# One order table for another: resequencing a fused attention and snake-MLP kernel

## The chip, the cores and the metric

The kernel runs on one core of one Trainium2 chip. The metric is device time in microseconds (us) of one execution; the number given for a kernel is the median over runs. TensorE, VectorE, ScalarE, GpSimd and SyncE appear as PE, DVE, ACT, POOL and SP; each works through its own instructions in order.

## The reference

Block-decayed linear attention (4 batches, 8 heads, 768 tokens, head size 64), whose output becomes the 3072 x 512 input of an MLP with a "snake" activation:

```
out_block   = (q k^T * Dmask) v + (q * lam_pow) @ kv_state     # per batch, head, block of tokens
kv_state    = lam_block * kv_state + (k * rev_pow)^T v
x           = out, heads side by side                          # 3072 x 512
h = x @ w_in                                                   # 512 -> 2048
s = sin(alpha * h)
g = h + s * s / (alpha + 1e-09)
return g @ w_out                                               # 2048 -> 512
```

All inputs and the result are float32; the kernel computes in bf16 with float32 accumulation.

## The kernel before, in words

Tokens are worked in six groups t = 0..5 of 128 tokens for all four batches, so a group is a 512-wide column block for the MLP. What a group needs is cut into small steps, and the whole body after a fixed preamble is a hand-held list of such steps, the string `ORDER` (line 14 on). A loop at line 491 reads the string word by word and records each step; nothing reorders them afterwards. A word is a letter, the indices (group first), and after a colon the PSUM banks that the step takes. Each engine's instruction stream is therefore the words in the string's order, filtered by the engine.

The letters, with the line of each function and its engine:

- `I1`..`I3` load a quarter of w_in (two DMAs each, L141) and `W0`..`W3` a quarter of w_out (one DMA each, L145). All are issued by POOL. The first quarter of w_in is loaded in the preamble (L187, four DMAs).
- `r` and `R` load raw k and raw q of a group (four DMAs each, L124), `n` and `v` load k and v in their natural layout (two DMAs each, L131), all issued by POOL. `d` decays k (L260) and `z` scales raw q (L264): POOL arithmetic. `C` casts the first state (L287, POOL).
- `k` and `j` turn raw k and raw q (L240, DVE). `F` computes scores into four banks (L249, PE), `m` masks one of them (L255, DVE). `K` computes state updates (L274, PE), `S` folds them in (ACT for group 0, L281; DVE otherwise, L283), `B` casts the state (L287, ACT). `O` computes attention outputs in four banks (L295, L304, PE), `x` copies one bank out as the MLP's input (L314, ACT).
- `h g.f:bank` is one of 16 "hidden" steps of a group: four 128x512 matmuls (L325). `s` takes the sine (L330, ACT). The square is `q` on ACT (L336), `Q` on DVE as a product (L338), or `P` on DVE as a fused form (L340). `t` finishes with a multiply-add into `gall` on DVE (L345), which also frees the bank.
- `u g.m.part:bank` is a quarter of an output projection: four matmuls (L352), of which part 0..3 uses the quarter 0..3 of w_out. `o` copies the finished bank out (ACT, L358) and stores it (SP, L360).

After the loop, line 494 calls `project_halves(5, 3)` (L362), which does the last projection in two halves of 256 columns, so that the first half is copied and stored while the second is computed.

Two things set what waits for what. PSUM has eight banks, and a step that names a bank waits for the reader of the bank's last content. And POOL's DMAs are recorded on eight semaphores in turn: a DMA issue carries a wait for the landing of the eighth DMA before it, and an issue that waits holds up whatever stands behind it on POOL. `raw_k` and `raw_q` have one buffer each, the natural k and v two each, the sine and the square four each, the output staging tile three.

Of the kernel before, what the change touches and what calls it, by code (L numbers as in the profile page):

```python
# [21 lines left out]
m1.0.1 u0.0.2 m1.0.2 u0.1.2 m1.0.3 r2 F1.1:2736 u0.3.1 m1.1.0 m1.1.1 u0.2.2 m1.1.2 u0.3.2 m1.1.3 O1:2736 v2  # L22
u0.0.3 x1.0 x1.1 u0.1.3 x1.2 x1.3 u0.2.3 z2.0 o0.0 o0.1 h1.0:2 o0.2 h1.1:7 s1.0 z2.1 j2.0 h1.2:3 q1.0 k2.0 s1.1
h1.3:6 s1.2 n1 t1.0 h1.4:4 q1.1 k2.1 q1.2 u0.3.3 s1.3 t1.1 s1.4 h1.5:5 n2 t1.2 o0.3 h1.6:0 q1.4 P1.3 s1.5 t1.4
F2.0:2713 s1.6 t1.3 r3 h1.7:4 q1.5 m2.0.0 q1.6 h1.8:6 m2.0.1 s1.7 m2.0.2 u1.0.0:2 q1.7 m2.0.3 s1.8 d1.0 u1.1.0:7
t1.5 q1.8 h1.9:1 t1.6 t1.7 d1.1 h1.10:3 s1.9 t1.8 h1.11:5 q1.9 j2.1 s1.10 h1.12:0 d2.0 s1.11 t1.9 q1.10 K1:46
s1.12 t1.10 h1.13:1 d2.1 q1.12 S1.0 h1.14:3 s1.13 S1.1 B1.0 u1.0.1 t1.12 B1.1 R3 q1.13 Q1.11 K2:46 t1.11 s1.14
h1.15:0 t1.13 q1.14 u1.1.1 S2.0 s1.15 v3 u1.0.2 t1.14 q1.15 B2.0 S2.1 F2.1:5143 t1.15 B2.1 u1.1.2 m2.1.0 n3
u1.0.3 m2.1.1 m2.1.2 z3.0 u1.1.3 o1.0 m2.1.3 u1.2.0:6 o1.1 k3.0 O2:0514 z3.1 j3.0 k3.1 u1.3.0:2 x2.0 x2.1 j3.1
u1.2.1 x2.2 x2.3 F3.0:3705 h2.0:1 m3.0.0 m3.0.1 h2.1:4 s2.0 m3.0.2 h2.2:3 q2.0 m3.0.3 s2.1 t2.0 h2.3:7 s2.2 d3.0  # L30
u1.3.1 q2.1 q2.2 t2.1 h2.4:0 s2.3 t2.2 d3.1 h2.5:5 q2.3 s2.4 t2.3 h2.6:1 s2.5 r4 q2.4 K3:43 q2.5 t2.4 h2.7:7
s2.6 t2.5 h2.8:0 q2.6 S3.0 R4 s2.7 h2.9:5 t2.6 B3.0 s2.8 h2.10:4 Q2.7 t2.7 s2.9 h2.11:1 S3.1 q2.8 v4 q2.9 u1.2.2
t2.8 B3.1 t2.9 h2.12:7 s2.10 k4.0 s2.11 u1.3.2 n4 q2.10 k4.1 u1.2.3 q2.11 s2.12 u1.3.3 t2.10 o1.2 t2.11 q2.12
z4.0 F3.1:3054 o1.3 t2.12 u2.0.0:6 m3.1.0 h2.13:1 m3.1.1 z4.1 u2.0.1 m3.1.2 s2.13 m3.1.3 h2.14:2 j4.0 O3:7305
s2.14 Q2.13 q2.14 t2.13 t2.14 u2.0.2 x3.0 d4.0 j4.1 x3.1 h2.15:4 x3.2 x3.3 F4.0:1273 s2.15 d4.1 h3.0:0 m4.0.0
q2.15 m4.0.1 h3.1:5 s3.0 t2.15 h3.2:1 q3.0 m4.0.2 s3.1 t3.0 K4:24 s3.2 m4.0.3 u2.0.3 q3.1 S4.0 q3.2 h3.3:7 t3.1
# [21 lines left out]
def kernel(  # L58
# [273 lines left out]
    def square(g, f, eng):  # L332
        s_sb = s_of.pop((g, f))
        s2_of[g, f] = mlps.tile([P, GRP], BF16, name="s2")
        if eng is A:
            A.activation(out=s2_of[g, f][:], in_=s_sb[:], func=ACTF.Square)  # L336
        elif eng is V:
            V.tensor_tensor(out=s2_of[g, f][:], in0=s_sb[:], in1=s_sb[:], op=ALU.mult)  # L338
# [9 lines left out]
    def project(g, m, part, n):  # L348
        if part == 0:
            ops[g, m] = bank("ops", n)  # L350
        for f in range(4 * part, 4 * part + 4):
            nc.tensor.matmul(out=ops[g, m][:], lhsT=gall[g][:, f, m * P:(m + 1) * P],  # L352
                             rhs=w_out_sb[part][:, f % 4, :],
                             start=(f == 0), stop=(f == NFC - 1))
# [170 lines left out]
```

## Time and profile before

| what | value |
|---|---|
| median of 3 runs | 211.4 us (210.08, 211.40, 212.85) |
| the profiled execution: its own time | 212.47 us |
| the profiled execution: span from first to last instruction | 210.8 us |
| PE busy | 197.1 us (94%) |
| ACT busy | 148.1 us (70%) |
| DVE busy | 135.7 us (64%) |
| POOL busy | 100.8 us (48%) |
| POOL's DMA queue: packets, bytes | 63184, 15.47 MB |

The profile is of one execution. Its own time is 1.7 us longer than its span (what lies around the first and the last instruction), and 1.1 us above the median of the three runs. Times in it count from the start of the span. Busy shares are averages over stages: the first 17 us are the preamble, in which PE turns and scores group 0 and waits for k, q, v and the first weights; then the MLP of group 0 runs while the weights still land; from about 53 us the steps of all later groups are mixed. For PE, 0.86 us is four 128x512 matmuls back to back at full clock, so one `h` or one `u` step. A matmul's listed duration (about 380 ns) contains the filling of the array and overlaps its neighbour's.

### The profile page before, as it was taken

What the parts mean: (1) busy time and instruction counts of PE and PEld (TensorE: products, weight loads), DVE (VectorE), ACT (ScalarE), POOL (GpSimd) and SP (SyncE); (2) the same over time, 40 slices, a digit from 0 to 9 for tenths busy, and PEclk for the clock granted to TensorE, in tenths of its full rate; (3) what the DMA queues carried; (4) which work ended last, traced back from release to release, by engine and by line L of the source; (5) the groups of instructions that cost most, each with busy time, mean ns of one, the idle gap of its engine ahead of it and who ended that gap; (6) DMA issues with size and microseconds to landing.
All of it is one profiled execution on the core that took longest, in us unless ns stands there. A gap on an engine that the chain in (4) does not pass through costs nothing.

```text
span 210.8 us, 4860 instructions
## 1 busy us (share of the span) xinstructions
PE 197.1 (94%) x1992; PEld 97.7 (46%) x2021; DVE 135.7 (64%) x201; ACT 148.1 (70%) x258; POOL 100.8 (48%) x116
## 2 busy tenths in 40 slices
...
GB/s 124 156 151 182 205 193 162 165 197 166 229 165 166 77 145 183 48 142 157 157 75 166 116 53 50 51 2 0 53 50 50 0 100 35 70 16 33 0 105 98
DMA packets 68920, 22.61 MB, mean 107 GB/s; under 512 B 50834, under 2 KB 65954, under 8 KB 68898
## 3 DMA queue, kind: packets, MB, share of 16 engines
q0 software_dynamic: 63184, 15.47, 79.6%
...
q14 instruction: 6, 0.05, 0.1%
...
## 4 chain that ended last, share of the span: by engine, by line
PE 74%; DMA 11%; DVE 5%; POOL 4%; ACT 2%; issue 2%; DVEq 0%; ACTq 0%; POOLq 0%
PE ops L352 35%; PE hps L325 29%; DMA w_in<-in_moe_w_in_dram 4%; DMA w_out<-in_moe_w_out_dram 4%; DMA nat_k<-in_k_dram 3%; PE F_ps L249 3%; PE O_ps L304 2%; DVE gall L345 2%; POOL nat_k L260 2%; DVE STm L255 2%; PE hps L367 2%; PE O_ps L295 2%; POOL w_in L141 1%; DVE S L283 1%; PE T_ps L387 1%
## 5 line engine op out<-in xcount | busy, mean ns | idle before, releaser
L345 DVE SCALAR_TENSOR_TENSOR gall<-s,r_sb,hps 128x512 bf16<-128x512 bf16 x96 | 69.3, 742 | 46.9 <-ACT s L336 36.8
L325 PE MATMUL hps<-xt,w_in 128*128 128x512 bf16 x372 | 90.9, 379 | 2.0 <-issue 0.7
L352 PE MATMUL ops<-w_out,gall 128*128 128x512 bf16 x352 | 88.1, 382 | 4.0 <-DMA w_out<-in_moe_w_out_dram 2.4
L330 ACT ACTIVATE s_sb<-hps,alpha_sb 128x512 bf16<-128x512 f32 x96 | 64.2, 692 | 27.7 <-PE hps L325 27.5
L325 PEld LDWEIGHTS <-w_in 128*128 128x128 bf16 x384 | 36.7, 98 | 46.0 <-issue 2.2
L352 PEld LDWEIGHTS <-gall 128*128 128x128 bf16 x368 | 35.1, 98 | 44.8 <-issue 3.7
L336 ACT ACTIVATE s<-s_sb 128x512 bf16<-128x512 bf16 x86 | 52.9, 638 | 1.6
L255 DVE TENSOR_TENSOR STm<-F_ps,C 128x512 bf16<-128x512 f32 x40 | 25.0, 683 | 4.2 <-PE F_ps L249 4.1
L260 POOL TENSOR_TENSOR nat_k<-nat_k,R 128x1024 bf16<-128x1024 bf16 x10 | 19.1, 1933 | 4.5 <-DMA nat_k<-in_k_dram 4.4
L264 POOL TENSOR_TENSOR raw_q<-raw_q,Rraw 128x1024 bf16<-128x1024 bf16 x10 | 18.9, 1919 | 4.0 <-DMA raw_q<-in_q_dram 4.0
L314 ACT CAST xt<-O_ps 128x512 bf16<-128x512 f32 x20 | 10.3, 600 | 14.9 <-PE O_ps L304 14.5
L358 ACT COPY o_sb<-ops 128x512 f32<-128x512 f32 x23 | 13.5, 592 | 8.0 <-PE ops L352 6.2
L240 DVE STREAM_TRANSPOSE turned_q<-raw_q 128x512 f32<-128x512 f32 x10 | 11.1, 1114 | 5.6 <-POOL raw_q L264 5.6
L131 POOL DMA_DIRECT2D nat_v<-in_v_dram x12 | 14.0, 1170 | 0.2 <-issue 0.2
L124 POOL DMA_DIRECT2D raw_k<-in_k_dram x20 | 11.7, 598 | 3.9 <-DMA w_out<-in_moe_w_out_dram 2.9
L124 POOL DMA_DIRECT2D raw_q<-in_q_dram x20 | 11.6, 588 | 4.0 <-DMA w_in<-in_moe_w_in_dram 2.6
L131 POOL DMA_DIRECT2D nat_k<-in_k_dram x10 | 11.8, 1190 | 0.8 <-POOLq L509 0.8
L240 DVE STREAM_TRANSPOSE turned_k<-raw_k 128x512 f32<-128x512 f32 x10 | 11.0, 1117 | 0.1
L338 DVE TENSOR_TENSOR s<-s_sb 128x512 bf16<-128x512 bf16 x9 | 5.9, 657 | 2.4 <-ACT s_sb L330 2.4
L249 PEld LDWEIGHTS <-turned_k 32*128 32x128 bf16 x320 | 5.0, 96 | 4.6 <-issue 3.8
L249 PE MATMUL F_ps<-turned_q,turned_k 32*128 32x128 bf16 x320 | 6.8, 224 | 0.0
L192 PE MATMUL spare<-fill 128*128 128x512 bf16 x11 | 5.0, 607 | 1.5 <-DVE one L174 1.5
...
## 6 DMA issues: line engine op xcount, KB each, us to landing
...
```

Of the source, the lines that this page charges most:

```text
L124: (eng or G).dma_start(out=dst[quad[a], bs].rearrange("t b n r d -> t (b n) (r d)"), in_=src[t, a])
L131: G.dma_start(out=nat[nm, t][:, bs].rearrange("p b h e -> p (b h) e"), in_=SRC[nm][bs, :, t * T:(t + 1) * T, :].rearrange("b h p e -> p (b ...
L240: V.transpose(out=dst.rearrange("p (x t r) -> p x r t", r=R, t=32), in_=src.rearrange("p (x r d) -> p x r d", r=R, d=32))
L249: nc.tensor.matmul(out=F[a][:, u, n, :], lhsT=KQ["k", t][quad[a], 2 * pr + u, n, :, e], rhs=KQ["q", t][quad[a], 2 * pr + u, n, :, e], star ...
L255: V.tensor_tensor(out=st[t, pr][:, a], in0=att["F", pr][a], in1=C0[:, a].unsqueeze(1).broadcast_to([P, 2, NQ, T]), op=ALU.mult)
L260: G.tensor_tensor(out=kd, in0=kd, in1=R128[:].unsqueeze(1).unsqueeze(3).broadcast_to([P, 2, H, D]), op=ALU.mult)
L264: G.tensor_tensor(out=qs, in0=qs, in1=Rraw[:].rearrange("p n r -> p (n r)").unsqueeze(1).unsqueeze(3).broadcast_to([P, 2, NQ * R, D]), op= ...
L325: nc.tensor.matmul(out=hps[g, f][:], lhsT=w_in_sb[f // 4][:, c, (f % 4) * P:(f % 4 + 1) * P], rhs=xt[g][:, c, :], start=(c == 0), stop=(c ...
L330: A.activation(out=s_of[g, f][:], in_=hps[g, f][:], func=ACTF.Sin, scale=alpha_sb[:, f:f + 1])
L336: A.activation(out=s2_of[g, f][:], in_=s_sb[:], func=ACTF.Square)
L345: V.scalar_tensor_tensor(out=gall[g][:, f, :], in0=s2_of.pop((g, f))[:], scalar=r_sb[:, f:f + 1], in1=hps.pop((g, f))[:], op0=ALU.mult, op ...
L352: nc.tensor.matmul(out=ops[g, m][:], lhsT=gall[g][:, f, m * P:(m + 1) * P], rhs=w_out_sb[part][:, f % 4, :], start=(f == 0), stop=(f == NF ...
```

## The change

`ORDER` is replaced as a whole by another list of the same steps, and the last projection becomes a step of the list (`e5.3:56`, the last word), with banks given in the word instead of 0 and 1. No instruction's shape changes. Counted over the two strings: the squares on ACT (`q`) go from 86 to 61, on DVE as a product (`Q`) from 9 to 15, on DVE in the fused form (`P`) from 1 to 20; all other letters keep their counts. The order of PE's steps and the banks differ nearly everywhere; so do POOL's steps.

POOL's steps in the order of the two strings, up to the loads of group 3:

```
before: I1 W0 d0.0 I2 d0.1 I3 r1 C0.0 C0.1 R1 W1 W2 v1 W3 z1.0 z1.1 R2 r2 v2 z2.0 z2.1 n1 n2 r3 d1.0 d1.1 d2.0 d2.1 R3
after:  d0.0 I1 I2 d0.1 r1 I3 R1 W0 W1 z1.0 W2 z1.1 v1 W3 C0.1 C0.0 r2 R2 n1 n2 z2.0 z2.1 d1.0 v2 d1.1 d2.0 R3 d2.1 r3
```

The diff, cut (the words on the left-out lines are of the same kinds):

```diff
 ORDER = """
-I1 W0 d0.0 I2 h0.0:2 d0.1 h0.1:4 s0.0 h0.2:5 s0.1 Q0.0 I3 t0.0 K0:73 s0.2 Q0.1 h0.3:6 S0.0 r1 t0.1 q0.2 C0.0
-h0.4:0 s0.3 t0.2 S0.1 h0.5:1 q0.3 h0.6:2 C0.1 s0.4 t0.3 s0.5 h0.7:7 R1 q0.4 u0.0.0:4 q0.5 t0.4 s0.6 u0.1.0:5
-t0.5 s0.7 Q0.6 h0.8:3 t0.6 h0.9:6 Q0.7 s0.8 t0.7 h0.10:0 s0.9 Q0.8 t0.8 W1 h0.11:1 s0.10 Q0.9 W2 h0.12:2 t0.9
-q0.10 s0.11 v1 t0.10 h0.13:7 s0.12 k1.0 h0.14:3 q0.11 q0.12 t0.11 h0.15:6 s0.13 W3 t0.12 s0.14 u0.2.0:0 k1.1
-q0.13 z1.0 u0.3.0:1 q0.14 t0.13 s0.15 t0.14 q0.15 z1.1 j1.0 u0.0.1 t0.15 u0.1.1 j1.1 F1.0:2736 R2 u0.2.1 m1.0.0
...
-q5.13 u5.1.0:3 t5.13 s5.14 h5.15:5 q5.14 t5.14 u5.1.1 s5.15 u5.2.0:7 q5.15 t5.15 u5.1.2 u5.0.3 u5.1.3 o5.0
-u5.2.1 o5.1 u5.2.2 u5.2.3 o5.2
+d0.0 h0.0:3 h0.1:5 h0.2:7 I1 s0.0 q0.0 s0.1 s0.2 t0.0 q0.1 I2 h0.3:6 q0.2 t0.2 h0.4:0 h0.5:1 t0.1 s0.3 s0.4 q0.3
+P0.4 d0.1 t0.4 r1 h0.6:4 h0.7:3 t0.3 s0.5 s0.6 s0.7 K0:52 S0.1 I3 P0.5 P0.6 t0.5 S0.0 R1 q0.7 t0.7 h0.8:2 s0.8
+h0.9:0 s0.9 W0 t0.6 q0.8 h0.11:6 k1.1 h0.10:7 q0.9 t0.9 s0.10 t0.8 h0.12:3 k1.0 s0.11 s0.12 q0.10 q0.11 q0.12
+h0.15:1 t0.10 t0.11 h0.13:0 s0.13 W1 h0.14:2 s0.14 t0.12 u0.1.0:7 u0.0.0:6 z1.0 j1.0 q0.13 q0.14 u0.2.0:4 t0.13
+t0.14 F1.0:2305 s0.15 q0.15 t0.15 u0.2.1 u0.1.1 W2 u0.3.0:1 u0.2.2 z1.1 j1.1 m1.0.1 m1.0.2 m1.0.3 m1.0.0
+F1.1:2530 u0.3.1 m1.1.0 v1 u0.0.1 W3 C0.1 C0.0 r2 u0.3.2 R2 m1.1.3 m1.1.2 m1.1.1 O1:2530 x1.0 x1.3 x1.1 k2.1
...
+t2.9 h2.11:1 s2.10 q2.10 t2.10 B2.1 d3.1 h2.12:4 r4 s2.11 s2.12 q2.11 u1.3.2 K3:20 k4.1 R4 m3.1.2 u1.3.3 o1.3
+h2.13:5 S3.1 O3:7360 S3.0 q2.12 t2.12 t2.11 s2.13 q2.13 u2.0.0:4 h2.14:1 z4.0 n4 j4.0 k4.0 t2.13 x3.0 x3.1 x3.2
...
+u2.1.2 k5.1 m4.1.1 s3.5 q3.5 t3.5 h3.6:4 s3.6 u2.3.1 u2.1.3 q3.6 k5.0 u2.3.2 K4:27 v5 o2.1 z5.0 O4:0136 x4.0
+t3.6 x4.3 u2.3.3 j5.1 o2.3 h3.7:0 x4.1 u2.2.0:6 S4.0 S4.1 h3.8:2 j5.0 s3.7 Q3.7 x4.2 t3.7 F5.0:1475 m5.0.0
...
+t3.11 h3.14:2 t3.12 s3.14 q3.14 B4.1 m5.1.1 t3.13 u3.0.1 u3.1.1 u3.0.2 t3.14 h3.15:0 s3.15 P3.15 u3.1.2 O5:3457
+x5.0 x5.1 x5.2 h4.3:2 x5.3 t3.15 h4.0:3 h4.5:4 s4.0 q4.0 h4.2:7 h4.1:5 s4.1 s4.2 u3.1.3 u3.0.3 o3.0 u3.3.0:0
...
+u5.0.2 s5.15 P5.15 u4.0.0:7 u5.1.1 u5.2.2 u5.1.2 t5.15 t5.14 u5.0.3 u5.2.3 o5.2 u5.1.3 o5.1 o5.0 u4.0.1 u4.0.2
+u4.0.3 o4.0 e5.3:56
 """
...
-    def project_halves(g, m):
+    def project_halves(g, m, *bks):
         for n in range(2):
             cols = slice(n * DM // 2, (n + 1) * DM // 2)
-            ps = bank("hps", n)
+            ps = bank("ops", bks[n])
...
+        "e": project_halves,
     }
     for word in ORDER.split():
         which, _, banks = word[1:].partition(":")
         STEP[word[0]](*map(int, which.split(".")), *map(int, banks))
-    project_halves(NT - 1, B - 1)
```

More of the change, by code (lines that the diff above doesn't have):

```diff
@@ L22 @@
[L22 to L36, printed above, removed]
@@ new lines @@
+t0.14 F1.0:2305 s0.15 q0.15 t0.15 u0.2.1 u0.1.1 W2 u0.3.0:1 u0.2.2 z1.1 j1.1 m1.0.1 m1.0.2 m1.0.3 m1.0.0
+F1.1:2530 u0.3.1 m1.1.0 v1 u0.0.1 W3 C0.1 C0.0 r2 u0.3.2 R2 m1.1.3 m1.1.2 m1.1.1 O1:2530 x1.0 x1.3 x1.1 k2.1
+x1.2 u0.1.2 k2.0 u0.2.3 n1 n2 u0.1.3 o0.1 o0.2 h1.0:0 s1.0 z2.0 P1.0 t1.0 h1.1:3 s1.1 z2.1 q1.1 h1.2:4 s1.2
+h1.3:2 s1.3 q1.2 t1.1 q1.3 t1.2 h1.5:7 j2.0 h1.4:5 s1.4 q1.4 t1.4 t1.3 u0.0.2 s1.5 q1.5 u0.3.3 t1.5 d1.0 u0.0.3
+j2.1 o0.3 h1.6:0 o0.0 h1.7:5 F2.0:7146 m2.0.1 m2.0.3 s1.6 h1.8:3 q1.6 s1.7 q1.7 t1.6 t1.7 h1.9:2 m2.0.0 m2.0.2
@@ new lines @@
+s1.8 s1.9 h1.15:1 q1.8 q1.9 v2 t1.8 h1.10:6 s1.10 h1.11:0 t1.9 q1.10 t1.10 h1.12:7 d1.1 K1:53 S1.0 d2.0 s1.11
+S1.1 h1.13:4 s1.12 q1.11 q1.12 u1.1.0:6 s1.13 q1.13 t1.11 R3 h1.14:5 u1.1.1 d2.1 t1.12 t1.13 s1.14 q1.14 t1.14
+F2.1:3027 m2.1.0 m2.1.1 B1.0 s1.15 m2.1.2 B1.1 q1.15 t1.15 u1.0.0:4 u1.1.2 u1.0.1 r3 K2:30 m2.1.3 u1.0.2 z3.0
+S2.1 j3.0 u1.1.3 o1.1 n3 O2:1275 x2.0 x2.2 x2.3 S2.0 x2.1 B2.0 k3.0 k3.1 u1.2.0:6 u1.0.3 u1.2.1 F3.0:2510 m3.0.0
+m3.0.3 o1.0 z3.1 v3 m3.0.2 h2.0:7 h2.1:3 s2.0 u1.2.2 m3.0.1 q2.0 t2.0 s2.1 q2.1 t2.1 h2.2:0 s2.2 j3.1 u1.2.3
@@ new lines @@
+o1.2 h2.3:5 h2.4:1 q2.2 t2.2 F3.1:2764 m3.1.0 s2.3 s2.4 h2.5:0 u1.3.0:3 h2.6:2 m3.1.3 q2.3 q2.4 t2.4 t2.3 s2.5
+m3.1.1 q2.5 t2.5 s2.6 h2.7:1 s2.7 q2.6 P2.7 t2.7 h2.8:4 s2.8 q2.8 u1.3.1 t2.6 t2.8 h2.9:7 s2.9 Q2.9 h2.10:5 d3.0
+t2.9 h2.11:1 s2.10 q2.10 t2.10 B2.1 d3.1 h2.12:4 r4 s2.11 s2.12 q2.11 u1.3.2 K3:20 k4.1 R4 m3.1.2 u1.3.3 o1.3
+h2.13:5 S3.1 O3:7360 S3.0 q2.12 t2.12 t2.11 s2.13 q2.13 u2.0.0:4 h2.14:1 z4.0 n4 j4.0 k4.0 t2.13 x3.0 x3.1 x3.2
+x3.3 u2.0.1 s2.14 F4.0:3762 m4.0.2 h2.15:0 q2.14 v4 m4.0.0 s2.15 q2.15 m4.0.1 z4.1 m4.0.3 d4.1 h3.1:5 h3.5:3
@@ new lines @@
+j4.1 h3.0:6 s3.0 s3.1 t2.15 u2.0.2 q3.0 t2.14 t3.0 h3.2:7 h3.3:2 u2.0.3 q3.1 t3.1 R5 r5 s3.2 P3.2 s3.3 q3.3
+u2.1.0:1 h3.4:6 t3.2 t3.3 B3.1 u2.1.1 o2.0 d4.0 z5.1 F4.1:4270 m4.1.3 m4.1.0 m4.1.2 s3.4 B3.0 q3.4 u2.3.0:5 t3.4
+u2.1.2 k5.1 m4.1.1 s3.5 q3.5 t3.5 h3.6:4 s3.6 u2.3.1 u2.1.3 q3.6 k5.0 u2.3.2 K4:27 v5 o2.1 z5.0 O4:0136 x4.0
+t3.6 x4.3 u2.3.3 j5.1 o2.3 h3.7:0 x4.1 u2.2.0:6 S4.0 S4.1 h3.8:2 j5.0 s3.7 Q3.7 x4.2 t3.7 F5.0:1475 m5.0.0
+m5.0.1 s3.8 Q3.8 h3.12:3 u2.2.1 t3.8 h3.9:4 s3.9 m5.0.3 u2.2.2 m5.0.2 h3.10:0 u2.2.3 B4.0 Q3.9 t3.9 s3.10 Q3.10
@@ new lines @@
+t3.10 F5.1:1524 m5.1.3 h3.13:7 o2.2 h3.11:0 s3.11 s3.12 m5.1.0 u3.1.0:6 u3.0.0:1 m5.1.2 Q3.11 Q3.12 s3.13 q3.13
+t3.11 h3.14:2 t3.12 s3.14 q3.14 B4.1 m5.1.1 t3.13 u3.0.1 u3.1.1 u3.0.2 t3.14 h3.15:0 s3.15 P3.15 u3.1.2 O5:3457
+x5.0 x5.1 x5.2 h4.3:2 x5.3 t3.15 h4.0:3 h4.5:4 s4.0 q4.0 h4.2:7 h4.1:5 s4.1 s4.2 u3.1.3 u3.0.3 o3.0 u3.3.0:0
+t4.0 q4.1 t4.1 u3.2.0:3 s4.3 P4.2 t4.2 u3.3.1 h4.6:5 h4.7:1 Q4.3 t4.3 u3.2.1 h4.4:2 s4.4 s4.5 P4.4 P4.5 t4.4
+s4.6 t4.5 s4.7 u3.3.2 u3.2.2 u3.3.3 o3.3 q4.6 t4.6 q4.7 t4.7 h4.8:7 u3.2.3 o3.2 s4.8 P4.8 h4.9:4 h4.11:2 h4.10:5
```

21 lines of the change are left out of this document (6 added, 15 removed).

## The prediction, on record before the changed kernel ran

> **What bounds the kernel now.** I read the page's chain first, then PE by stages, then the chain of the first 55 us, then POOL's timeline, last DVE's and ACT's groups.
>
> ```profile
> PE 74%; DMA 11%; DVE 5%; POOL 4%; ACT 2%; issue 2%; DVEq 0%; ACTq 0%; POOLq 0%
> ```
> ```profile
> core 0: us, PE busy (x) PEld busy (x) DVE busy (x) ACT busy (x) POOL busy (x), PEclk, DMA share, GB/s
> 16.80:52.80 36.00, 32.23 (x343) 15.28 (x350) 23.79 (x34) 19.31 (x34) 27.34 (x34) 0.95 1.43 182
> 52.80:207.50 154.70, 153.00 (x1535) 75.27 (x1555) 99.54 (x140) 118.26 (x203) 58.24 (x54) 1.00 0.69 87
> ```
> PE is the bound, and from 52.8 us on it has no slack to give: 153.0 of 154.7 us busy at full clock. What can still be won lies between 16.8, where the first hidden step starts, and 52.8. The chain there:
>
> ```profile
> 20.67 8.87 DMA w_in<-in_moe_w_in_dram
> ...
> 30.48 7.97 DMA w_out<-in_moe_w_out_dram
> 38.45 0.04 issue
> 38.49 2.37 PE ops L352 x8
> 40.85 0.97 PE F_ps L249 x27
> ```
> PE stands still for the second quarter of w_out (W1), issued at 30.5 and landed at 38.45: PE's wait is 2.39 us. The eight matmuls after it take 2.37 us and not 1.73: the clock is halved. The windows of 3.41 us around it:
>
> ```profile
> 12.45:15.87 3.42, 2.08 (x49) 1.59 (x48) 3.05 (x6) 2.49 (x5) 3.35 (x5) 1.00 1.63 155
> 36.35:39.76 3.41, 1.27 (x6) 0.58 (x6) 2.51 (x4) 0.68 (x2) 2.96 (x2) 1.00 1.29 165
> 39.76:43.17 3.41, 3.08 (x38) 1.50 (x38) 2.00 (x4) 0.00 (x0) 2.44 (x5) 0.50 2.24 168
> ```
> A stretch with PE busy for 1.27 of 3.41 us (37%) is followed by one at clock 0.50; one with 2.08 (61%) is not.
>
> ```profile
> 14.15 0.83 POOL L145 DMA_DIRECT2D w_out<-in_moe_w_out_dram  x1
> 21.27 1.76 POOL L124 DMA_DIRECT2D raw_k<-in_k_dram  x3
> 30.48 0.78 POOL L145 DMA_DIRECT2D w_out<-in_moe_w_out_dram  x1
> 31.73 0.75 POOL L145 DMA_DIRECT2D w_out<-in_moe_w_out_dram  x1 [0.47 <-issue]
> 34.74 0.78 POOL L145 DMA_DIRECT2D w_out<-in_moe_w_out_dram  x1
> 45.23 0.58 POOL L124 DMA_DIRECT2D raw_k<-in_k_dram  x1 [1.00 <-DMA nat_v<-in_v_dram]
> 47.88 0.58 POOL L124 DMA_DIRECT2D raw_k<-in_k_dram  x1 [2.08 <-DMA w_out<-in_moe_w_out_dram]
> ```
> W0 is issued at 14.2, W1 to W3 from 30.5 on. Adding each issue's start to its time to landing gives the landings: w_in quarter 1 at 21.2, W0 23.5, w_in 2 27.2, w_in 3 29.5, raw k (four) 32.2, raw q (four) 34.9, W1 38.45, W2 41.6, nat v 44.9, W3 47.6. They land in the order of issue with hardly a gap, so the queue itself is full, and the pitches are prices: w_in pair 2.3 to 3.7, four raw loads 2.7, a w_out 2.3 to 3.5, two nat_v 3.4.
>
> **PE's balance before.** By the chain's rows four 512-wide matmuls are 0.86 us. 96 hidden and 92 projection steps are 188 x 0.864 = 162.4; the halves 3.5; ten F of 0.61, five K of 0.62, five O of 1.70 give 17.7. Together 183.6. PE ends at 207.5: 207.5 - 16.8 - 183.6 = 7.1 us of loss. By the start of group 1's hidden steps (52.86) the string has 30.3 us of PE work: loss 5.8 up to there, 1.3 after. The span ends 3.3 after PE, and the execution takes 1.7 beyond its span.
>
> **The change, part by part.**
>
> *Same work on PE.* All step counts of PE are kept: 183.6 again. The preamble is untouched: start at 16.8, first w_in quarter at its old place.
>
> *POOL's issues.* W0 moves from ahead of d0.0 to behind raw q: 12 DMAs (w_in 2 and 3, eight raw loads) go past it. raw k goes ahead of w_in 3. d0.0 moves ahead of w_in 1 and delays that issue by one tensor operation, 1.9 us: 14.9 instead of 12.95, plus the shortest w_in time to landing, 5.0, is 19.9 against 19.6 for its first half, so +0.3 at most. The DMAs ahead of W2 are the same set in both strings, only shuffled: with a full queue W2 lands at 41.6 again, nat v at 44.9, W3 at 47.6. (W2 now waits on POOL behind z1.0, which waits for raw q: 32.6 + 1.9 = 34.5, and by the shortest w_out time, 8.0, that would be 42.5; range 41.6 to 42.5.) raw q's landing is the old 34.9 less W0's 2.3: 32.6. W0 follows it by 2.3 to 3.5: 34.9 to 36.1; two middle pitches of 3.1 back from W2 give 35.4, which I take, and W1 at 38.5. w_in 3 lands four raw loads before raw q's end: 29.9.
>
> *PE up to W0.* The string now puts all 16 hidden steps and K0 (14.5 us) before the first projection. The last four hidden need w_in 3: 29.9 + 3.5 = 33.4. The waits ahead of that hide under it: w_in 1 lets h0.4 start at 21.5, and four hidden, K0 (0.6), the copy S0.1 (0.6 plus handing over) that h0.8 must wait for, since it takes K0's own bank 2, and four hidden more are done at 29.8. Without w_in 3 as cover that bank's turn would cost its 0.7. PE then waits for W0 from 33.4 to 35.4: 2.0 us in place of the 2.39 for W1. ACT does not set this: 13 squares and 16 sines in pairs of about 1.16 and 1.26 us, and two copies, from 17.9 on are 18.8, done at 36.7, and the banks that u0.1.0 and u0.0.0 take are free at about 33.7.
>
> *The clock.* If that wait falls into one 3.41 us stretch, PE is busy 41% of it: nearer to the 37% that was followed by the half clock than to the 61% that was not. I take the halving; it stretches what PE does in the 3.4 us behind it by 1.7. The Trainium skill ("TensorE: Matmul & The Clock Gate", section "Why this matters for your kernels") asks only that no idle gap exceed about 3 us; by it neither 2.39 nor 2.0 should have cost clock. The trace disagrees for the 2.39.
>
> *W0 to group 1.* From 35.4 seven steps up to u0.2.2 are 5.8 us: 41.2, or 42.9 at half clock; W2 (41.6) then no longer stops PE. At u0.2.2 the string has 20.2 us of PE work: loss 42.9 - 16.8 - 20.2 = 5.9, or 4.6 unhalved (W2's 41.6). F1.1 to O1 has four masks (0.62 apart) inside three projections (2.6), as before. So 5.9 against 5.8 before.
>
> *POOL for group 2.* n1, n2 go ahead of z2, and v2, r3 behind d1. The last raw q issue of group 2 waits for the eighth DMA before it, W3 (47.6, as the 2.08 row shows), and lands about 5.1 later, 53; then z2 (3.8), d1.0, v2 (2.3), d1.1 end at 62.9. K1 is needed at 16.8 + 5.9 + 43.9 = 66.6: covered by 3.7 us. F2.0 (60.8) has its z2.0 at 54.9, K2 (73.9) its d2.1 at 69.0. No cost; if the cover went, POOL's lateness would come out on PE one for one. SP's stores keep count and order of copies.
>
> *Squares.* ACT loses 25 of 0.630: -15.8 us. DVE gains 19 fused of 0.684 and 6 products of 0.418, and no longer meets POOL's arithmetic with products (two of nine took 1.16 and 1.82): about +13.
>
> ```profile
> L338 DVE TENSOR_TENSOR s<-s_sb x9: 418/419/1824, 18.6 to 103.1; 128x512 bf16<-128x512 bf16 x9
> L345 DVE SCALAR_TENSOR_TENSOR gall<-s,r_sb,hps x96: 677/747/749, 20.4 to 198.5; 128x512 bf16<-128x512 bf16 x96
> ```
> ACT goes to 132, DVE to 149, both under PE's 190 us: nothing. The multiply-adds lie between 677 and 749 ns all 96 times, while POOL runs 1.9 us tensor operations at 20 places: the distance kept from those has nothing to win.
>
> *Bank turns later.* Counted over the strings in PE work between a bank's last write and its next use, the shortest before is 1.46 us (u1.2.3 to u2.0.0). After, three are 0.86: u1.3.3 to O3, O4 to h3.7, O5 to h4.0. The copies that free them take 0.585, and O writes its first bank 0.8 us before its end, so the lower end is 0; the upper, 1.1 each, is under the rivals. I take 0.5 together.
>
> *Tail.* The halves get banks 5 and 6, free long before; 3.3 us as before.
>
> **Sum.** Loss 5.9 + 1.3 + 0.5 = 7.7 against 7.1: +0.6 on the profiled 212.47, so 213.1. That execution stands 1.1 above its median of 211.4; put on the median, 212.0 us.
>
> **Rivals.**
>
> *No halved clock* (the wait is split over two stretches, or W0 lands at 34.9, leaving PE busy 56%): loss 4.6 + 1.8 = 6.4, 1.3 less: 210.7. That is also where the skill's 3 us rule leads. Chance 0.25.
>
> *Weights early:* W0 34.9, W2 39.6 (34.5 plus the 5.1 of the fastest raw load): loss 3.6 and 1.3, 2.2 under before: 209.2. Against it: the full queue. Chance 0.05; a gain over 2% needs 4.2 of the 7.1 and is 0.02 of it.
>
> *W0 lands where W1 did* (38.5, if raw loads are served ahead of it more slowly, POOL being late with each): 38.5 - 16.8 - 14.5 = 7.2, halving 1.7, later 1.8: 10.7, +3.6: 215.0. It decides from a landing of about 36.5. Chance 0.12, half of it over 2%.
>
> *Bank turns (the slower side).* At O3, O4 and O5 one ACT instruction stands ahead of the freeing copy. The only row of this kind before is PE's 0.4 us wait for an o_sb copy, at distances of 1.46 to 1.73; at 0.86 it would be 0.4 + 0.7 = 1.1 each, 3.3 in all; and if two such waits leave PE under some 45% of a stretch, 1.7 more: 212.0 - 0.5 + 5.0 = 216.5. The Trainium skill (same page, section "A second HAM failure mode: psum-queue depth-cycling") describes such a loss of clock through bank turns; before, from 43.2 on, the clock is 1.00 throughout. Chance 0.16, 0.10 of it over 2%.
>
> *It does not do what its name says:* W0 is issued later, not first, and the distances from POOL act on DVE, off the chain. That is inside the forecast.
>
> **How the numbers follow.** Forecast 212.0 with chance 0.42, its own range 211 to 213.5. The range 209.0 to 216.4 takes in early weights, late W0 and most of the bank turns. What a measurement here can tell is about 2%, so 207.2 to 215.6 is no change: faster 0.02, slower 0.06 + 0.10 = 0.16, same 0.82.
>
> **What would show it.** W0 landing near 35.4 and PE waiting about 2 us for w_out, now for W0; one stretch at clock 0.50 behind it; group 1's first hidden step within 1 us of 51.3 (28.6 of work, 16.8, 5.9); PE over 98% busy from there on; ACT near 132 and DVE near 149. Wrong if PE shows waits for ACT's L314 or L358 after 90 us, a second stretch at half clock, or w_out landings in another order than issued.

## The result and the profile after

| what | before | after |
|---|---|---|
| median of 22 runs each, on the same chip | 210.92 us (209.68 to 213.14) | 213.18 us (212.07 to 214.74) |
| ratio | | 1.011, 95% interval 1.0088 to 1.0131 |
| the profiled execution: its own time, its span | 212.47 us, 210.8 us | 212.93 us, 211.1 us |
| PE busy | 197.1 us | 196.5 us |
| ACT busy, DVE busy | 148.1 us, 135.7 us | 134.0 us, 148.5 us |

The changed kernel is slower by 1.1%, some 2.3 us. The forecast was 212.0 us and no change: the time lies inside the range, but it is a small loss that the runs do separate from no change. Ratios and their intervals leave out executions over 1.5% longer than the fastest of the same kernel, so a ratio need not be the quotient of the medians beside it.

The profile after is read in the order of the prediction. First the page's chain by engine, and PE by stages, cut where group 1's hidden steps are under way (the columns of a stage are given in its first line):

```profile
PE 63%; DMA 14%; POOL 12%; DVE 6%; issue 3%; ACT 1%; POOLq 0%; DVEq 0%; ACTq 0%
```
```profile
core 0: us, PE busy (x) PEld busy (x) DVE busy (x) ACT busy (x) POOL busy (x), PEclk, DMA share, GB/s
16.80:51.30 34.50, 31.71 (x341) 15.07 (x347) 21.93 (x32) 20.87 (x38) 25.31 (x32) 0.95 1.33 178
51.30:207.50 156.20, 153.56 (x1538) 75.81 (x1558) 114.18 (x168) 102.57 (x175) 60.51 (x55) 1.00 0.71 89
```

From 51.3 us on PE is busy for 153.56 of 156.20 us (98.3%). POOL now holds 12% of the chain that ended last, against 4% before. Where it stands in that chain is seen in the chain of the first 60 us (start, duration, what):

```profile
25.78 7.22 DMA raw_q<-in_q_dram
...
33.16 1.90 POOL raw_q L264
35.06 0.77 POOL w_out L145
...
35.84 1.92 POOL raw_q L264
37.76 2.28 POOL nat_v L131 x2
40.04 8.32 DMA w_out<-in_moe_w_out_dram
48.36 0.04 issue
48.41 1.89 PE ops L352 x8
50.29 5.18 PE hps L325 x24
```

The third and the fourth quarter of w_out (W2, W3) are issued between and behind the two halves of `z1`, and `z1.0` waits for raw q, which lands at 33.00. So W3 goes out at 40.04 and lands at 48.36, and the projection step that needs it starts 0.05 us later. In this execution PE was hardly early for it: the profile lists no wait there. PE's own timeline shows what came of the predicted wait for W0 (start, duration, what, and in brackets the idle time ahead of it and what ended that):

```profile
35.43 2.76 PE L352 MATMUL ops<-w_out,gall 128*128 128x512 bf16 x12 [1.36 <-DMA w_out<-in_moe_w_out_dram]
...
100.04 0.73 PE L295 MATMUL O_ps<-turned_q,Sb 32*64 32x128 bf16 x61 [0.43 <-DVE S L283]
...
120.98 0.68 PE L274 MATMUL KV_ps<-nat_v,nat_k 128*32 128x64 bf16 x64 [0.47 <-DVE STm L255]
```

The wait for W0 is 1.36 us. The other two lines are waits for DVE, at `O3` and `K4`, that the prediction did not have. They are read from DVE's timeline, first around `O3` and then around `K4`:

```profile
94.27 2.07 DVE L338 TENSOR_TENSOR s<-s_sb 128x512 bf16<-128x512 bf16 x1
...
99.22 1.42 DVE L283 SCALAR_TENSOR_TENSOR S<-S,L,KV_ps 128x512 f32<-128x512 f32 x2
...
119.04 1.17 DVE L240 STREAM_TRANSPOSE turned_k<-raw_k 128x512 f32<-128x512 f32 x1 [1.14 <-DMA raw_k<-in_k_dram]
119.99 0.73 DVE L255 TENSOR_TENSOR STm<-F_ps,C 128x512 bf16<-128x512 f32 x1
```

The square `Q2.9` takes 2.07 us instead of 0.42, while POOL's `z4` runs (94.15 to 96.05 on POOL's timeline), and the state update that `O3` needs (99.22) comes behind it. At 119 the turn `k5.1` stands idle for raw k of group 5, which landed at 118.85 (at 112.15 in the profiled execution before), and the mask `m4.1.1` that frees `K4`'s bank stands behind that turn.

**The balance.** Loss is PE's time less its work, as in the prediction: the start of group 1's first hidden step less 16.8 and the work the string has ahead of it, then PE's end less 200.4. After: 50.29 - 16.8 - 28.6 = 4.9, and with PE's end at 207.85 (chain) 7.45, so 2.6 later on. The prediction's sum was 5.9 and 1.8.

### The profile page after: what moved, and what is told of

The parts are those of the page before. It is cut to its first block, busy times and chain, and to the rows that moved or that the text cites. A ratio compares the mean times of both kernels' runs of the same rounds, so it can differ in the third digit from the quotient of the medians.

```text
span 211.1 us, 4862 instructions
## 1 busy us (share of the span) xinstructions
PE 196.5 (93%) x1994; PEld 97.2 (46%) x2021; DVE 148.5 (70%) x226; ACT 134.0 (63%) x233; POOL 101.1 (48%) x116
## 4 chain that ended last, share of the span: by engine, by line
PE 63%; DMA 14%; POOL 12%; DVE 6%; issue 3%; ACT 1%; POOLq 0%; DVEq 0%; ACTq 0%
PE ops L352 28%; PE hps L325 27%; DMA w_out<-in_moe_w_out_dram 4%; DMA w_in<-in_moe_w_in_dram 4%; DMA raw_q<-in_q_dram 3%; DMA raw_k<-in_k_dram 3%; POOL nat_v L131 2%; POOL w_in L141 2%; PE F_ps L249 2%; PE O_ps L304 2%; POOL raw_q L264 2%; DVE STm L255 2%; POOL raw_q L124 2%; PE ops L367 2%; DVE gall L345 1%
## 5 line engine op out<-in xcount | busy, mean ns | idle before, releaser
L325 PE MATMUL hps<-xt,w_in 128*128 128x512 bf16 x371 | 89.7, 384 | 2.6 <-DVE xt L416 0.9
L352 PE MATMUL ops<-w_out,gall 128*128 128x512 bf16 x355 | 85.2, 379 | 2.8 <-DMA w_out<-in_moe_w_out_dram 1.4
L330 ACT ACTIVATE s_sb<-hps,alpha_sb 128x512 bf16<-128x512 f32 x96 | 63.1, 685 | 35.4 <-PE hps L325 34.5
L345 DVE SCALAR_TENSOR_TENSOR gall<-s,r_sb,hps 128x512 bf16<-128x512 bf16 x96 | 67.9, 742 | 16.1 <-ACT s L336 15.2
L325 PEld LDWEIGHTS <-w_in 128*128 128x128 bf16 x384 | 37.2, 99 | 47.0 <-issue 4.3
L336 ACT ACTIVATE s<-s_sb 128x512 bf16<-128x512 bf16 x61 | 37.2, 630 | 0.9
L255 DVE TENSOR_TENSOR STm<-F_ps,C 128x512 bf16<-128x512 f32 x40 | 25.5, 684 | 6.8 <-PE F_ps L249 6.8
L358 ACT COPY o_sb<-ops 128x512 f32<-128x512 f32 x23 | 13.1, 587 | 15.6 <-PE ops L352 15.4
L340 DVE SCALAR_TENSOR_TENSOR s<-s_sb 128x512 bf16<-128x512 bf16 x20 | 13.4, 688 | 11.3 <-ACT s_sb L330 11.3
L314 ACT CAST xt<-O_ps 128x512 bf16<-128x512 f32 x20 | 10.5, 598 | 15.3 <-PE O_ps L304 15.3
L338 DVE TENSOR_TENSOR s<-s_sb 128x512 bf16<-128x512 bf16 x15 | 8.0, 532 | 3.9 <-ACT s_sb L330 3.7
```

Source lines behind the costliest of these rows:

```text
L255: V.tensor_tensor(out=st[t, pr][:, a], in0=att["F", pr][a], in1=C0[:, a].unsqueeze(1).broadcast_to([P, 2, NQ, T]), op=ALU.mult)
L325: nc.tensor.matmul(out=hps[g, f][:], lhsT=w_in_sb[f // 4][:, c, (f % 4) * P:(f % 4 + 1) * P], rhs=xt[g][:, c, :], start=(c == 0), stop=(c ...
L330: A.activation(out=s_of[g, f][:], in_=hps[g, f][:], func=ACTF.Sin, scale=alpha_sb[:, f:f + 1])
L345: V.scalar_tensor_tensor(out=gall[g][:, f, :], in0=s2_of.pop((g, f))[:], scalar=r_sb[:, f:f + 1], in1=hps.pop((g, f))[:], op0=ALU.mult, op ...
```

## The theories

*A, the yardstick.* The one profiled execution of before was a dear one: its wait for W1 and the half clock behind it are not what this kernel usually has. Its loss of 7.1 is then too high a base, and the 1.1 us taken off at the end belong to before alone, not to both kernels.

*B, the early loads.* W0's wait is new, and W2, v1 and W3 are issued late because they stand on POOL behind `z1`. (This is about the issues: W2 landed at 40.90, before the 41.55 of the first profile.)

*C, the later order.* `K4`'s mask behind a turn that waits for raw k, and the square that meets POOL's arithmetic, cost what the prediction did not look for.

The expectations quoted below were written before this lettering: theory B of e2 belongs to C here, and theory C of e3 and e4 is that the early and the late part each have a share.

*Rivals:* the squares on DVE, which were put at nothing, make the kernel slower; or it is one part of the new string, early or late, that a splice with the old one would take away whole.

## The experiments

Ratios are against the kernel before on the same chip. The runs were made on several chips, so medians of different rows are compared through their ratios. The kernel after is at 1.011 (1.0088 to 1.0131). Diffs are in the words of the order string.

| run | median us (lowest to highest) | ratio, 95% interval | profiled execution's own time |
|---|---|---|---|
| e1_before_again | 210.64 (209.73 to 212.23) | 1.0032 (0.9999 to 1.0065) | 210.32 |
| a0_after_again | 213.16 (211.64 to 213.81) | 1.0111 (1.0025 to 1.0196) | 213.81 |
| e2_no_meet | 214.26 (212.59 to 216.16) | 1.0171 (1.0112 to 1.0230) | 212.82 |
| e3_early_before | 213.14 (211.35 to 213.84) | 1.0126 (1.0078 to 1.0174) | 213.57 |
| e4_early_after | 218.62 (216.00 to 226.77) | 1.0351 (1.0291 to 1.0412) | 216.27 |
| b1_w1_before_rawq | 212.06 (210.91 to 216.52) | 1.0069 (1.0029 to 1.0109) | 214.25 |
| p1_old_issue_order | 216.12 (212.30 to 220.09) | unclear, no interval | 214.44 |
| m1_late_mended | 213.16 (212.19 to 216.37) | 1.0106 (1.0012 to 1.0199) | 216.37 |
| c1_w_ahead | 212.37 (211.51 to 213.42) | 1.0085 (1.0055 to 1.0114) | 211.51 |
| c2_mask_first | 213.25 (212.26 to 213.72) | 1.0126 (1.0085 to 1.0167) | 213.10 |
| c3_new_mended | 211.29 (210.93 to 219.12) | 1.0040 (1.0012 to 1.0067) | 212.34 |
| c4_old_early_mended | 214.08 (212.50 to 215.86) | 1.0142 (1.0078 to 1.0206) | 214.67 |
| d1_late_only | 213.46 (212.12 to 214.01) | 1.0104 (1.0066 to 1.0141) | 214.01 |
| d2_squares_back | 214.60 (213.36 to 215.38) | 1.0173 (1.0135 to 1.0210) | 214.39 |

### Theory A: the kernel before, profiled again

No edit.

> The kernel before, unchanged, for a second profile of it. Theory A (the profiled execution of before was one with a halved clock behind the wait for W1, and most are not): ratio 1.000, and if this profile shows no stretch at clock 0.50 behind PE's wait for w_out, PE's loss falls from 7.1 to about 5.4 us and the span from 210.8 to about 209. Rival (the halving is in every execution): the half clock at about 40 us is there again and the span is 210.5 to 211.

This execution took 210.32 us. Its PE has no wait for W1 at all. The chain of its early part (start, duration, what) runs over DVE, not over a load:

```profile
31.10 0.75 DVE gall L345
31.84 0.34 DVE s L338
32.21 0.66 DVE gall L345
...
33.53 1.12 DVE turned_k L240
34.66 1.25 DVE gall L345 x2
35.91 1.02 DVE turned_k L240
...
50.72 2.37 PE hps L325 x11
```

W1 was issued 1.4 us earlier than in the first profile (29.05 against 30.48) and landed at 36.27 instead of 38.45; W3 landed at 45.73. Group 1 starts at 50.72: loss 50.72 - 16.8 - 30.3 = 3.6, and with PE's end at 205.36 5.0 in all, against 5.8 and 7.1. So theory A holds: two microseconds of what was to be won or kept were the chance of one execution. The 22 runs agree, as 18 of them are shorter than the profiled one (212.47). With this base the prediction's own sum for after (7.7) would have been +2.7 instead of +0.6. This second execution is itself 0.6 us below the median of the 22; taken up to that median, the base is some 5.6 (an estimate) and the sum +2.1. How often before has the wait is not known: c4 below, with the same early words, shows it again.

The kernel after, once more, shows how far its waits wander:

> The changed kernel unchanged, as the yardstick for the other runs on this chip: ratio 1.009 to 1.013 to before. PE waits for W0 (landing 35.4) and once more ahead of K4.

It landed W0 at 35.58 (PE waited 1.15 us), stood 0.78 us for W2, which landed at 42.39, and 1.40 us at `K4`. At `O3` it did not wait. The wait for W0 and the one at `K4` are there again, with other sizes.

### Splices: early and late part apart

e3 has the old string up to group 1's first hidden step and the new one from there on (banks renumbered to fit), e4 the reverse.

> The old string up to the first hidden step of group 1, then all other words in the order of the new string, its banks renumbered to fit. Theory C (the early part, with W0 behind raw q, costs about 0.6 to 1 us against an undisturbed execution of before, the later part 1.2): this has the later cost alone, ratio 1.005 to 1.007. Rival (all of the loss is early): 1.000. Rival (all is later): 1.011.

> The new string up to the first hidden step of group 1, then all other words in the order of the old string, banks renumbered. Theory C: the early cost alone, ratio 1.003 to 1.005. Rival (all early): 1.011. Rival (all later): 1.000. In the profile W0 should land near 35.4 and PE wait for it as in the changed kernel.

Neither told the halves apart. In e3 the early loss is small (W1 at 36.65, a wait of 0.71), but `K4` then waits 2.45 us for its mask, and a wait of 1.43 at 56.5 comes from the splice itself: a multiply-add that frees a bank stands on DVE behind turns of group 2, whose raw k is late. In e4 the old later part finds its loads too late and `F2.0` and the hidden step behind it stand still four times between 59.5 and 63.6 (0.83, 0.44, 0.42 and 1.35 us). A later part needs the load order that its own early part issued. c4, a second splice, with the later mends below and with `z2.1`, `k2.0` and `k2.1` moved to where the old early part can serve them, fared no better:

> The old string up to group 1, then the new string with the mask first, square 2.9 on ACT, and, against what the splice itself did, z2.1 ahead of n1 and the turns k2 behind t1.0 and t1.1. Theory (early part and K4 are the whole loss): level with before, ratio 0.997 to 1.003, PE's loss near 4.7 us. Rival (the new later part is dearer all along, through bank turns at 0.86 us): 1.004 or more with PE's waits at O3, O4 or O5.

Its profile has W1 at 37.84, a wait of 2.55 us for it with the half clock behind, and 1.22 us at 59.2 from the splice. These three are inconclusive as to halves.

### Theory B: the early issues

p1 keeps the new order on PE, ACT and DVE and puts POOL's early steps back into the old one:

```diff
-d0.0 ... I1 ... I2 ... d0.1 r1 ... I3 ... R1 ... W0 ... W1 ... z1.0 ... W2 ... v1 ... W3
+I1 W0 d0.0 I2 ... d0.1 I3 r1 ... R1 ... W1 W2 v1 W3 ... z1.0
```

> The changed kernel with GpSimd's steps up to the scaling of group 1's raw q in the old order (W0 right behind w_in 1, raw k and q behind w_in 3, W1 to W3 ahead of the scaling); PE's order stays new. Theory (the new issue order makes all of w_out late): W0 lands near 23, W1 at 36 to 38, W3 at 46 to 47.5; the 1.4 us wait for W0 goes, a shorter one for the first scores or W1 takes its place, 0.8 to 1.5 us less than the changed kernel. Rival (PE's new order, 16 hidden steps and then projections, costs it whatever the weights do): less than 0.4 us.

W0's wait is gone (W0 landed at 23.76), and another has its place. PE's timeline in p1:

```profile
34.17 1.89 PE L323 MATMUL hps<-xt,w_in 128*128 128x512 bf16 x8 [1.79 <-DVE gall L343]
36.35 2.75 PE L350 MATMUL ops<-w_out,gall 128*128 128x512 bf16 x12 [0.30 <-DVE gall L343]
39.86 0.64 PE L247 MATMUL F_ps<-turned_q,turned_k 32*128 32x128 bf16 x32 [0.76 <-DVE gall L343]
```

DVE's timeline in p1:

```profile
32.49 1.09 DVE L238 STREAM_TRANSPOSE turned_k<-raw_k 128x512 f32<-128x512 f32 x1 [2.73 <-DMA raw_k<-in_k_dram]
33.45 1.32 DVE L343 SCALAR_TENSOR_TENSOR gall<-s,r_sb,hps 128x512 bf16<-128x512 bf16 x2
```

(Line numbers are two lower in the rewrapped strings of the experiments.) The new order turns raw k early on DVE, and the multiply-add that frees a bank stands behind that turn. With W0 back in front, raw k lands at 32.37 and not at 26.87, and PE waits 1.79 us for the bank. So the new place of W0 is the price of the early turns, and undoing it alone brings another wait in place of the 1.36 us. Whether the kernel is slower for it is not shown: its four runs lie between 212.30 and 220.09, too far apart to tell. b1 tries the like on the kernel before: W1 ahead of raw q.

```diff
-R1 q0.4 ... W1 h0.11:1
+W1 R1 q0.4 ... h0.11:1
```

> The kernel before with W1 issued ahead of group 1's raw q. If PE's wait for W1 (2.39 us in the first profile, 0 to 0.7 in the later two) and the half clock behind it are what spreads before's runs from 209 to 213: W1 lands 2.7 us earlier, no wait, no half clock behind it, median 0.5 to 1 us less and fewer runs over 211.5. Rival: raw q, 2.7 to 3.4 us later, makes F1.0 or F1.1 late instead, and the time is the same or up to 1 us more.

W1 landed at 35.11, raw q later at 37.59, and `F1.0` waited 2.70 us (38.03 to 40.73) for its turn: 0.7% slower. What came forward in this queue pushed the next load back.

c1 is the one early edit that costs no other load its place: W2, v1 and W3 only go ahead of POOL's arithmetic.

```diff
-z1.0 j1.0 ... W2 ... z1.1 ... v1 ... W3
+W2 v1 W3 z1.0 j1.0 ... z1.1
```

> The changed kernel with W2, nat v and W3 issued ahead of z1.0 on GpSimd, where it now stands idle for 5 us until raw q lands; all else kept. Theory (the three loads queue on GpSimd behind an arithmetic step that waits for raw q, so the DMA queue runs dry and W3 lands at 48.3 to 50.1 in place of 45.7 to 46.6): W3 lands near 46.5, PE's waits for W2 and W3 (0 to 2.0 us by execution) go, the wait for W0 stays; 0.5 to 1 us less than the changed kernel, ratio 1.006 to 1.009. Rival (the queue is full anyway and only the issue moves): landings and time unchanged, 1.011.

POOL's timeline and, in the second fence, the same rows of the kernel after:

```profile
28.98 0.75 POOL L143 DMA_DIRECT2D w_out<-in_moe_w_out_dram  x1 [0.90 <-DMA w_in<-in_moe_w_in_dram]
30.67 2.29 POOL L129 DMA_DIRECT2D nat_v<-in_v_dram  x2 [0.94 <-DMA w_in<-in_moe_w_in_dram]
32.94 0.77 POOL L143 DMA_DIRECT2D w_out<-in_moe_w_out_dram  x1
33.71 3.79 POOL L262 TENSOR_TENSOR raw_q<-raw_q,Rraw 128x1024 bf16<-128x1024 bf16 x2
```
```profile
33.16 1.90 POOL L264 TENSOR_TENSOR raw_q<-raw_q,Rraw 128x1024 bf16<-128x1024 bf16 x1 [5.11 <-ACT s L336]
35.01 0.81 POOL L145 DMA_DIRECT2D w_out<-in_moe_w_out_dram  x1
35.84 1.92 POOL L264 TENSOR_TENSOR raw_q<-raw_q,Rraw 128x1024 bf16<-128x1024 bf16 x1
37.70 2.36 POOL L131 DMA_DIRECT2D nat_v<-in_v_dram  x2
40.04 0.77 POOL L145 DMA_DIRECT2D w_out<-in_moe_w_out_dram  x1
```

W3 is issued at 32.94 instead of 40.04, and landed at 46.34 instead of 48.36 (the row of after puts its 5.11 us of idle time down to a square on ACT; the chain above shows that raw q, landed at 33.00, ended it). PE has no wait for W3, and none at `K4` either, where raw k of group 5 landed at 117.37. There is none at `O3`: `z4.0` started at 93.20 and not at 94.15, and the product that meets it took 1.40 us:

```profile
93.97 1.40 DVE L336 TENSOR_TENSOR s<-s_sb 128x512 bf16<-128x512 bf16 x1
```

What W3's lateness costs differs by execution. Of the eight profiles that issue it behind `z1`, two list no wait for it (after, a0), and the others 0.30 (e2), 0.64 (d2), 0.77 (e4), 0.96 (c2), 1.33 (d1) and 1.97 us (m1). With c1's issues it landed at 46.34 (c1) and 46.48 (c3), without a wait. PE's steps stand in the same order in c1 and after, so the same weight load can be compared in time: c1's comes 0.3 us earlier at the end of W3's projection, 1.0 behind `O3`, 1.5 at `K4` and 1.3 from there to the end. That is c1's shortest execution (211.51). By the ratios the gain is 0.25%, some 0.5 us. The two intervals overlap, so the sign is likely and not shown by this run alone.

### Theory C: the later waits, one by one

e2 gives the square 2.9 the fused form (`Q2.9` to `P2.9`). c2 puts the mask `m4.1.1` ahead of the turn `k5.1`. m1 does both and issues raw k of group 5 ahead of its raw q.

```diff
-... h2.9:7 s2.9 Q2.9 ... R5 r5 ... u2.1.2 k5.1 m4.1.1
+... h2.9:7 s2.9 P2.9 ... r5 R5 ... u2.1.2 m4.1.1 k5.1
```

> The changed kernel with one square, group 2 number 9, in the fused form on DVE in place of the product, which took 2.07 us beside GpSimd's scaling of raw q. Theory B (that late product delays the state update S3.1 on DVE, for whose bank O3 waits): the square takes 0.68, PE's idle time before O3 (0.43 us of wait and 0.42 us of late weight loads) goes, 0.8 to 1.0 us less than the changed kernel: ratio to before 1.006. Rival (DVE has slack there and O3 waits for something else): ratio stays 1.011.

> The changed kernel with three words of the later part moved: the mask m4.1.1 ahead of the turn k5.1 on DVE, raw k of group 5 issued ahead of raw q, and square 2.9 in the fused form. Theory (K4 waits for a bank whose mask stands on DVE behind a turn that waits for raw k; O3 waits for a state update behind a product that met GpSimd): both of PE's waits, ahead of O3 and K4, go, 1.3 to 1.7 us less than the changed kernel. Rival (the loss sits in the early part alone): no change beyond 0.5 us, and PE waits as long elsewhere.

> The changed kernel with one word moved: m4.1.1 ahead of k5.1 on DVE. Theory (K4's bank is freed by that mask, which stands behind a turn that waits for raw k of group 5): PE's wait ahead of K4 (0.5 to 2.5 us by execution) goes and nothing takes its place: 0.8 to 1.4 us less than the changed kernel, ratio 1.005 to 1.007. Rival (PE then waits as long at O4 or F5.0): 1.011.

None of them gained: 214.26 (e2), 213.16 (m1) and 213.25 us (c2). What e2 and c2 were to take away was gone in their own profiles, though. In e2's the square took 0.68 us, `O3`'s wait is gone and PE gained 0.8 us there on after's execution, while `K4`'s wait was 0.78; why e2's other runs are longer than its profiled one (212.82) is not shown. In c2's `K4`'s wait is gone, while `O3` waited 0.42 us and W3's projection 0.96. In m1's profile `K4`'s wait is gone, but the fused square now met POOL's arithmetic, which the fused form was to avoid. DVE's row in m1:

```profile
97.67 2.06 DVE L338 SCALAR_TENSOR_TENSOR s<-s_sb 128x512 bf16<-128x512 bf16 x1
```

POOL's row at the same time:

```profile
97.28 1.90 POOL L262 TENSOR_TENSOR raw_q<-raw_q,Rraw 128x1024 bf16<-128x1024 bf16 x1 [5.32 <-DMA raw_q<-in_q_dram]
```

So it is not the form of the square that is held up; `O3` still waited 0.43 us there. (That execution was the dearest of m1's runs, with W3 landing at 50.09 and a half clock behind PE's wait for it.) c3 puts 2.9 on ACT instead, with c2's mask and c1's loads:

```diff
-... z1.0 j1.0 ... W2 ... v1 ... W3 ... s2.9 Q2.9 ... k5.1 m4.1.1
+... W2 v1 W3 z1.0 j1.0 ... s2.9 q2.9 ... m4.1.1 k5.1
```

> Both edits together, and square 2.9 on ACT, so that neither of its inputs is read beside GpSimd's arithmetic: what is left of the loss against before is W0's wait. Theory: 1.8 to 2.5 us less than the changed kernel, ratio 1.000 to 1.003, loss of PE 5 to 5.5 us. Rival (each mended wait comes out elsewhere): above 1.007.

211.29 us, ratio 1.0040: of the 1.1%, 0.4% is left, some 1.5 us less, and the interval is clear of after's. d1 is c3 without c1's loads:

> The new order with only the two late mends (mask m4.1.1 ahead of the turn k5.1, square 2.9 on ACT) and with W2, v1, W3 left behind z1.0. If the late waits are worth 1.1 us by themselves (as with the early loads moved: 212.37 to 211.29), this gives about 212.1, ratio near 1.007. If they pay only when the loads run early (each later load shifts the next wait), it stays at about 213, ratio 1.010 to 1.012, and POOL's loads of group 5 land as late as in the new kernel (raw k after 118.5).

213.46 us: nothing gained. Two rows of its PE timeline show what PE waited for behind W0:

```profile
50.06 1.89 PE L350 MATMUL ops<-w_out,gall 128*128 128x512 bf16 x8 [1.33 <-DMA w_out<-in_moe_w_out_dram]
...
122.80 0.74 PE L293 MATMUL O_ps<-turned_q,Sb 32*64 32x128 bf16 x62 [0.62 <-DVE gall L343]
```

The first is W3, which landed at 50.02. For the second, DVE's timeline shows what that multiply-add stood behind:

```profile
121.07 1.14 DVE L238 STREAM_TRANSPOSE turned_k<-raw_k 128x512 f32<-128x512 f32 x1 [1.70 <-DMA raw_k<-in_k_dram]
122.08 0.67 DVE L343 SCALAR_TENSOR_TENSOR gall<-s,r_sb,hps 128x512 bf16<-128x512 bf16 x1
```

Raw k of group 5 landed at 120.88 there. With the mask out of the way, the next thing behind the turn is a multiply-add, and it frees the bank that `O4` takes. So a wait at `K4` was handed on to `O4`: both stand behind a turn on DVE that waits for a late load. Compared with after's execution at the same weight loads, d1 lost 1.2 us at W3, gained 0.8 at `O3` and 0.5 at `K4`, and lost 0.8 at `O4`. So the two mends did act, but part came back at once, and a dear W3 outweighed the rest. In c1 and c3, where raw k of group 5 landed at 117.37 and 117.97, neither `K4` nor `O4` waits. By the ratios, late mends alone give 0.06% (1.0104 against 1.0110), early loads alone 0.25%, both 0.7%. The first two intervals overlap after's, so it is likely, and not shown, that each mend needs the other. The gain of both together is shown.

### The rival: the squares on DVE

d2 gives the 20 fused squares back to ACT and leaves the rest.

```diff
-P0.4 ... P5.15
+q0.4 ... q5.15
```

> The new order with its 20 fused DVE squares given back to ACT (ACT 81 squares, DVE 15 products); order, banks and loads unchanged. If the share of squares on DVE is worth nothing, as the prediction put it: 213.2, ratio 1.009 to 1.013, ACT about 147 us busy and DVE about 135. If ACT then delays sines and bank copies: 214 or more, with PE waiting for ACT's sine or copies. If the DVE squares themselves are what made the new kernel slower: 212 or less.

214.60 us, ratio 1.0173, interval 1.0135 to 1.0210, clear of after's: slower by another 1.3 us. PE's waits (in us, times, longest) begin with these:

```profile
PE hps L323 <- ACT S L279: 1.3, 1, 1.3
PE ops L350 <- DMA w_out<-in_moe_w_out_dram: 1.2, 2, 0.6
```

`h0.8` waited 1.28 us for the state copy `S0.1`, which stands on ACT behind more squares (0.76 in the kernel after). This did not cost anything: the wait for W0 behind it shrank from 1.36 to 0.53 us, and the first projection started at 35.44, as in after (35.43). What stayed are delays of 0.5 us at `F1.0`, for a bank that a multiply-add frees, 0.5 at W3, which landed at 49.55, 0.5 at `F5.0`, and 0.6 late in the kernel; 0.8 was won at `O3`. The late one is ACT's, by PE's and DVE's rows:

```profile
180.71 1.02 PE L323 MATMUL hps<-xt,w_in 128*128 128x512 bf16 x4 [0.40 <-DVE gall L343]
```
```profile
179.91 0.75 DVE L343 SCALAR_TENSOR_TENSOR gall<-s,r_sb,hps 128x512 bf16<-128x512 bf16 x1 [3.02 <-ACT s L334]
```

The rival falls: in this string the fused squares on DVE save some 0.6%, 1.3 us. They are not why the kernel is slower. Where the 1.3 us are saved is shown only in part.

## Why the prediction was right and where it was wrong

*PE's work* is the same by count in both strings (183.6 us). PE was busy for 98.3% of the later stretch, where over 98% was said, and ACT 134.0 and DVE 148.5 us against 132 and 149.

*POOL's early issues* were right up to W0: it landed at 35.38 (35.4 predicted) and W1 at 37.89. W0 was also late enough to matter: PE waited 1.36 us, not 2.0, because the hidden steps ended at 34.07 and not 33.4 (a wait of 0.76 us for `S0.1` that was to lie under w_in). That wait ended at 27.01; in c1, which has no half clock in its early part, it ended at 25.49 and did lie under w_in.

*"with a full queue W2 lands at 41.6 again, nat v at 44.9, W3 at 47.6"* failed for W3, and in its premise. The set of loads ahead was the same, and W2 was even early (40.90). But POOL handed out v1 and W3 between tensor operations, and the pitch grew: v1 landed at 45.31, 4.4 us behind W2, where it took 3.4 before and in c1. W3 landed at 48.36 here and between 48.3 and 50.1 in seven further profiles with these issues (a0, e2, e4, c2, m1, d1, d2), against 47.60 and 45.73 in the two profiles of the kernel before. The text saw W2 behind `z1.0` and gave it a bound; it did not carry that to v1 and W3.

*The half clock behind W0's wait* did not come. Here the windows of the clock's grid:

```profile
13.80:17.21 3.41, 1.35 (x18) 0.85 (x20) 2.69 (x5) 0.93 (x2) 3.41 (x5) 1.00 1.13 144
34.28:37.69 3.41, 2.26 (x11) 1.08 (x12) 3.27 (x6) 3.18 (x6) 3.39 (x3) 1.00 1.03 149
```

PE was busy for 2.26 of 3.41 us (66%) around the wait, and the clock stayed whole. The halved stretch of this execution lies at 17.2 to 20.6, behind a window with 1.35 (40%). It cost nothing: c1's execution had none there, and at the first projection step both stand at a loss of 4.1 us (35.4 - 16.8 - 14.5), as W0's landing sets that time. The term of 1.7 us in the sum was wrong; group 1 started at 50.29, not 51.3 (1.0 us early, at the edge of what the prediction allowed), for this reason. Its unhalved figure was a loss of 4.6, and the late W3 made it 4.9.

*POOL for group 2, no cost,* held for group 2, and stopped there. The order of the loads of groups 3 to 5 was not followed, and raw k of group 5 at 118.85, behind raw q in the new order, is where `K4` waits.

*The squares at nothing* were wrong in both directions. They save about 1.3 us in this string (d2), and one product still met POOL's arithmetic (2.07 us), although the text said that it no longer would. *Bank turns* were put at 0.5 for ACT's copies at `O3`, `O4` and `O5`. No wait for L314 or L358 showed there. PE's later waits, 0.43 and 0.47 us in the profile, are for DVE.

*The step that failed is the last one:* "That execution stands 1.1 above its median of 211.4; put on the median, 212.0". The sum on the profiled execution, 213.1, came within 0.2 us of that kernel's profiled execution (212.93), and its loss of 7.7 within 0.3. The 1.1 us were taken off after as well, although they came from a wait for W1 and a half clock that the change removes, and that before's second profile does not have. So the term that failed is the base, the loss of 7.1: the second profile showed 5.0, and some 5.6 at the median of the 22 runs. Set against these, the own sum meant +2.7 or +2.1 us; measured were 2.3. Part of that agreement is luck: 1.7 us of halving that was not there stood in for 0.8 us of further waits later on and for 0.3 us of the lateness of W3.

*What stays open.* c3 is still 0.4% behind before. The wait for W0 (1.47 us in c3's profile, none for W1 in before's second one) would account for it, but this is argued: the run that took the wait away (p1) brought another. c3's profiled execution, 1.05 us above its median, also stood 0.76 us inside `F5.0`, and its trace does not tell for what.
